# Forty-eight products that nobody reads, placed in TensorE's waits in the early slots of an RWKV-7 and squared-ReLU kernel

## The chip, the cores and the metric

One core of one Trainium2 chip. The metric is the device time of one execution in microseconds (us). The kernel before and a changed kernel are run alternately on the same chip. One traced execution of each kernel gives the profile. Its span (first to last instruction) is about 1.7 us shorter than the time of the same execution.

## The reference

Inputs `r, k, v, w, a, b` have the shape (4, 8, 768, 40): 4 sequences, 8 heads, 768 steps, 40 channels, float32.

```python
for t in range(S):
    y[:, :, t] = einsum('bhd,bhde->bhe', r_t, state)
    Sa = einsum('bhde,bhe->bhd', state, a_t)
    state = state * w_t[:, :, None, :] - einsum('bhd,bhe->bhde', Sa, b_t) + einsum('bhd,bhe->bhde', v_t, k_t)
# (B,H,S,D) -> x of 3072 x 320
h = maximum(x @ w_in, 0)          # 320 -> 2048
out = (h * h) @ w_out             # 2048 -> 320
```

## The kernel before

The sequence is cut into 24 pieces of 128 steps, which I call slots: 6 chunks of each of the 4 sequences. Slots 0 to 3 are the first chunk of each. A slot is `chain(i)`: a row of small products, each of which needs the last one's result copied out of PSUM. Other work is woven in between: preparing later slots (`early`, `rest`), rounding the second set of weights (slots 0 and 1), and from slot 2 the feed-forward network (`ffn`).

The part that the change touches, cut:

```python
def chain(i, g):
    ...
    x_ = by_head(psum(ps_c))                              # bank 1 of 2
    for h in range(H):
        mm(x_[:, h], g["A"][h % 2][:, h // 2], v_[:, h, :D], h == 0)
    ...
    nc.scalar.copy(xr[first], x_[first])
    yield
    xs = by_head(psum(ps_c))                              # bank 2 of 2
    for h in range(H):
        mm(xs[first, h], T[first, order_of(h)], xr[first, h], h == 0)
    nc.scalar.copy(xn[first, :, :D], xs[first])
    yield
    for h in range(H):
        mm(x_[second_, h], N[:, order_of(h)], xn[first, h, :D], False)
    nc.scalar.copy(xr[second_], x_[second_])
    yield
    for h in range(H):
        mm(xs[second_, h], T[second_, order_of(h)], xr[second_, h], h == 0)
    nc.scalar.copy(xn[second_, :, :D], xs[second_])
    yield
    p_ = psum(ps_c)
    for q in range(NP):
        nc.tensor.transpose(p_[:, q * 128:(q + 1) * 128], pair(xn, q), ident)
    ...                       # state, masks; the last products are RV,in_k and RX,in_b into y_
```

Each `yield` lets the weave put other work in. Some names that the profile uses: `dec` is a slot's table of decays, stored by `early` and loaded back by `rest`; `decay` is the same table while it is made for a later slot; `A`, `RV` and `RX` are products that VectorE multiplies with a triangular mask; groups named `ident,...` are transposes, and `ps_c<-ident` alone is a group of the new products; `RX,in_b` is the last product of a slot. A clock that is down, or cold, is at 0.50; full is 1.00. `T` comes from an inversion on GpSimd, once for two or four slots (`solve`). Its input is loaded by the same queue as the stores that end a slot, and behind them (in the trace before, the stores of slot 3 are issued from 299.62 us on, the loads of `half_n` from 302.57):

```python
store(t_[row:row + m_, j], t_[at:at + m_, NT], 1)      # end of chain: the token stores, four of them
...
nc.sync.dma_start(out=part[...], in_=kept[...])         # solve: loads half_n from kept_d
```

Of the kernel before, what the change touches and what calls it, by code (L numbers as in the profile page):

```python
# [17 lines left out]
def kernel(  # L18
# [24 lines left out]
    B, H, S, D = r.shape  # L43
# [26 lines left out]
    ps_c = ctx.enter_context(tc.tile_pool(name="ps_c", bufs=2, space=PSUM))  # L70
    ps_f = ctx.enter_context(tc.tile_pool(name="ps_f", bufs=2, space=PSUM))

    def psum(pool):
        name = "ps_" + pool.name[-1]
        return pool.tile([128, 512], FP32, tag=name, name=name)

    def mm(o, l_, r_, start):
        nc.tensor.matmul(o, l_, r_, start=start, stop=True, skip_group_check=True)  # L78

    def single(name, shape):  # L80
        return const.tile(shape, FP32, tag=name, name=name)

    def new(name, shape, bufs):
        return work.tile(shape, FP32, tag=name, name=name, bufs=bufs)
# [4 lines left out]
    def later(fn, steps=2):  # L89
        line.append([steps, fn])  # L90
# [7 lines left out]
    def store(out_, in_, steps=2):  # L98
        later(lambda: nc.sync.dma_start(out=out_, in_=in_), steps)  # L99

    quads = lambda t_: t_.rearrange("p (q t) -> p q t", q=NP)
    by_head = lambda t_: t_[:, :DM].rearrange("t (h d) -> t h d", h=H)
# [43 lines left out]
    ident = single("ident", [128, 128])  # L146
# [136 lines left out]
    def masked(name, bufs, l_, r_):  # L283
        res = []
        for p_ in products(l_, r_):
            t_ = new(name, [128, NP, 128], bufs)
            nc.vector.tensor_tensor(t_, p_, over4(upper), Alu.mult)  # L287
            res.append(t_)
        return res
# [150 lines left out]
    def chain(i, g):  # L440
        bb, c = order[i]
        st = states.tiles[bb]
        aT, rT, k_, b_, v_, T, N = (g[x] for x in ("aT", "rT", "k", "b", "v", "T", "N"))
        sd = g.get("sd")
        first, second_ = slice(0, HC), slice(HC, C)
        x_ = by_head(psum(ps_c))
        for h in range(H):
            mm(x_[:, h], g["A"][h % 2][:, h // 2], v_[:, h, :D], h == 0)
        if c > 0:
            for q in range(NP):  # L450
                mm(x_[:, 2 * q:2 * q + 2], aT[:, q], st[:, q, :, :D], False)
        xr = new("xr", [128, H, D], 1)
        nc.scalar.copy(xr[first], x_[first])
        yield
        xn = minus_x.next()
        xs = by_head(psum(ps_c))
        for h in range(H):
            mm(xs[first, h], T[first, order_of(h)], xr[first, h], h == 0)
        nc.scalar.copy(xn[first, :, :D], xs[first])
        yield  # L460
        for h in range(H):
            mm(x_[second_, h], N[:, order_of(h)], xn[first, h, :D], False)
        nc.scalar.copy(xr[second_], x_[second_])
        yield
        for h in range(H):
            mm(xs[second_, h], T[second_, order_of(h)], xr[second_, h], h == 0)
        nc.scalar.copy(xn[second_, :, :D], xs[second_])
        yield
        p_ = psum(ps_c)
        for q in range(NP):  # L470
            nc.tensor.transpose(p_[:, q * 128:(q + 1) * 128], pair(xn, q), ident)  # L471
        xT = turned("xnT", 1)
        nc.scalar.copy(xT, quads(p_))
        yield
        if c < NCH - 1:
            grown = psum(ps_c)[:, :NP * 2 * D].rearrange("p (q e d) -> p q e d", q=NP, e=2)
            for q in range(NP):
                mm(grown[:, q], pair(k_, q), v_[:, 2 * q:2 * q + 2, :D], q == 0)
            for q in range(NP):
                mm(grown[:, q], pair(b_, q), xn[:, 2 * q:2 * q + 2, :D], False)  # L480
            nc.vector.tensor_tensor(st[:, :, :, :D], grown, st[:, :, :, :D], Alu.add)
            ended[bb] = new(f"end{bb}", [128, NP], 1)
            nc.vector.tensor_copy(ended[bb], g["up"][:, :, C])
            yield
        rx = masked("RX", 2, xT, rT)
        yield

        y_ = quads(psum(ps_c))
        if c > 0:
            for q in range(NP):  # L490
                mm(y_[:, q], sd[:, q].rearrange("p e d -> p (e d)"), rT[:, q], q == 0)
        for m_, rows in ((g["RV"], k_), (rx, b_)):
            for q in range(NP):
                for e in range(2):
                    mm(y_[e * DP:(e + 1) * DP, q], rows[:, 2 * q + e, :], m_[e][:, q], c == 0 and q == 0 and rows is k_)
        n = i % GB
        if n == 0:
            tokens[i // GB] = new("tokens", [128, NP, GB * C], 2)
        t_ = tokens[i // GB][:, :, n * C:(n + 1) * C]
        nc.vector.tensor_tensor(t_, y_, g["up"][:, :, :C], Alu.mult)  # L500
        for j, row, h, d, m_ in gaps:
            at = (h % 2) * DP + d
            store(t_[row:row + m_, j], t_[at:at + m_, NT], 1)
        if n == GB - 1:
            later(lambda: gathered.add(i // GB), 2)
        yield
# [113 lines left out]
    for i in range(len(order)):  # L620
        bb, c = order[i]
        n, ahead = share.get(i, (TOTAL, 0))
        for _ in range(ahead):
            next(second)
            tick()
        tc.no_sync_barrier()
        parts = [(chain(i, ready.pop(i)), 9, 0, TOTAL)]
        if 1 < i + 1 < len(order):
            load(i + 1)
            ready[i + 1] = {}  # L630
            parts.append((rest(i + 1, ready[i + 1]), 9, 2, TOTAL))
        if i < B:
            parts += [(prepare(B + 2 * i), 5, 0, TOTAL - 5), (prepare(B + 2 * i + 1), 5, 5, TOTAL)]
        elif i + LEAD < len(order):
            parts.append((prepare(i + LEAD), 5, 0, TOTAL - 2))
        if i < 2:
            parts.append((some(rounding, 8 - 4 * i), 8 - 4 * i, 0, TOTAL))
        parts.append((some(second, n), n, 0, TOTAL))
        weave(*parts)
# [34 lines left out]
```

## Time and profile before

| | before |
|---|---|
| median of 4 runs beside the change | 1188.46 us (1185.67 to 1190.74) |
| span of the traced execution | 1177.1 us |
| busy: TensorE, VectorE, ScalarE, GpSimd | 85%, 42%, 20%, 62% |
| mean clock granted to TensorE | 0.917 |

The traced execution was shorter than any of the four timed ones.

Two habits of reading help here. First, the clock column gives the clock that the trace knows of, and in the first 100 us it says 1.00 although the products take their slow time: a group of 16 for `ps_w<-dec,kvT` takes 2.08 us at 67.86 us, and 1.16 us where the clock is full. The duration of a known group is the safer thermometer. Second, the bracket at the end of a timeline line gives TensorE's idle time before the group, and who ended it.

### The profile page before, as it was taken

To read this page: it belongs to the slowest core of one execution; us is meant where nothing else is said; L and a number is where in the kernel's file an instruction comes from. 1 tells how busy PE (TensorE), PEld (TensorE's weight loads), DVE (VectorE), ACT (ScalarE), POOL (GpSimd) and SP (SyncE) were. 2 spreads that over 40 slices of the span, in tenths; PEclk is the share of its full clock that TensorE was granted. 3 is DMA by queue.
4 is the path that set the end of the run, shared out by engine and by line. 5 is a ranking of instruction groups with operands and counts; after the bars stand their busy time and mean duration, and the time that the engine had idled before them with its cause. 6 is when DMAs were issued, how large, how long until landed. Compare 5 with 4: busy or idle time off the path is not lost.

```text
span 1177.1 us, 18561 instructions
## 1 busy us (share of the span) xinstructions
PE 999.4 (85%) x7248; PEld 829.6 (70%) x7248; DVE 491.1 (42%) x1008; ACT 233.5 (20%) x511; POOL 731.4 (62%) x1085
## 2 busy tenths in 40 slices
PE   4232477889999899429999989999989999999998
PEld 3121466778788687318888878788778887888886
DVE  6289576354354155005525424544233242322211
ACT  1033121211221122002112112122122121221211
POOL 4687886488488699979997059994089990000000
PEclk9997556879989899859999989999999999999999
DMA  7946645747655934244663394354353421433000
GB/s 113 169 135 182 137 110 125 146 104 160 152 99 101 170 70 86 48 94 98 109 105 101 86 155 78 87 113 101 92 90 66 77 52 51 76 64 76 3 13 12
DMA packets 261992, 114.95 MB, mean 98 GB/s; under 512 B 243472, under 2 KB 248464, under 8 KB 260368
## 3 DMA queue, kind: packets, MB, share of 16 engines
q1 hardware_dynamic: 256704, 96.98, 43.3%
q10 hardware_dynamic: 4048, 10.49, 3.1%
q0 software_dynamic: 1152, 6.29, 1.4%
q8 instruction: 57, 0.93, 0.4%
q14 instruction: 31, 0.25, 0.1%
HBM read 77.34 MB, written 35.40 MB: 96 GB/s over the span
## 4 chain that ended last, share of the span: by engine, by line
PE 61%; POOL 9%; DVE 5%; DMA 4%; SPq 2%; issue 1%; ACT 0%; POOLq 0%; DVEq 0%; ACTq 0%
PE ps_f L78 34%; PE ps_c L78 16%; PE ps_w L78 6%; POOL half_t L354 5%; POOL half_p L352 4%; PE ps_w L271 4%; DMA dec<-kept_e 2%; DMA T<-kept_t 1%; SPq L133 1%; PE ps_c L428 1%; SPq L99 1%; PE ps_c L471 1%; DVE RV L287 1%; PE ps_w L418 1%; DMA half_n<-kept_d 1%
## 5 line engine op out<-in xcount | busy, mean ns | idle before, releaser
L352 POOL TENSOR_TENSOR half_p<-half_n,half_t 128x252 f32<-128x252 f32 (+52 forms) x504 | 333.6, 662 | 169.6 <-DMA half_n<-kept_d 130.6
L354 POOL TENSOR_TENSOR half_t<-half_t,half_p 128x252 f32<-128x252 f32 (+52 forms) x504 | 366.1, 726 | 39.5
L78 PE MATMUL ps_f<-tokens,w_in 128*128 128x256 f32 x1152 | 293.1, 399 | 0.0
L523 DVE TENSOR_TENSOR hid<-ps_f,hid 128x256 f32<-128x256 f32 x192 | 80.8, 421 | 412.9 <-ACT hid L522 412.8
L78 PEld LDWEIGHTS ps_f<-tokens,w_in 128*128 128x128 f32 x1152 | 216.0, 198 | 31.2 <-issue 0.4
L78 PE MATMUL ps_f<-w_out,hid 128*128 128x320 f32 x768 | 221.0, 437 | 0.0
L78 PEld LDWEIGHTS ps_f<-w_out,hid 128*128 128x128 f32 x768 | 140.7, 190 | 53.9 <-issue 0.2
L522 ACT ACTIVATE hid<-ps_f 128x256 f32<-128x256 f32 x192 | 73.8, 384 | 244.9 <-PE ps_f L78 244.9
L78 PE MATMUL ps_c<-xr,T 64*64 64x40 f32 x768 | 59.4, 239 | 54.1 <-DMA T<-kept_t 52.7
L78 PEld LDWEIGHTS ps_c<-xr,T 64*64 64x64 f32 x768 | 53.7, 147 | 70.3 <-issue 68.2
L78 PEld LDWEIGHTS ps_c<-in_v,A 128*128 128x128 f32 x384 | 50.5, 206 | 17.1 <-DVE w_out L230 14.7
L78 PE MATMUL ps_c<-in_v,A 128*128 128x40 f32 x384 | 49.1, 290 | 14.3 <-DVE w_out L230 14.3
L78 PE MATMUL ps_w<-dec,kvT 40*128 40x128 f32 x384 | 32.4, 316 | 27.3 <-DVE kvT L394 27.2
L78 PEld LDWEIGHTS ps_w<-dec,kvT 40*128 40x128 f32 x384 | 27.3, 215 | 32.2 <-DVE kvT L394 29.2
L78 PE MATMUL ps_w<-decay,bT 40*128 40x128 f32 x352 | 36.8, 340 | 15.4 <-DVE decay L312 13.8
L319 ACT COPY N<-ps_w 128x512 f32<-128x512 f32 x48 | 25.8, 589 | 119.6 <-PE ps_w L78 71.9
L500 DVE TENSOR_TENSOR tokens<-ps_c,dec 128x512 f32<-128x512 f32 x24 | 16.5, 686 | 72.6 <-PE ps_c L78 70.7
L271 PE MATMUL ps_w<-ident,in_w 128*128 128x128 f32 x96 | 19.1, 333 | 32.4 <-DMA in_w<-in_w_dram 31.0
L78 PEld LDWEIGHTS ps_w<-decay,bT 40*128 40x128 f32 x352 | 31.3, 237 | 21.0 <-issue 12.9
L287 DVE TENSOR_TENSOR RX<-ps_w,upper 128x512 f32<-128x512 f32 x48 | 30.8, 682 | 27.0 <-PE ps_w L78 27.0
L78 PEld LDWEIGHTS ps_c<-minus_x,N 64*64 64x64 f32 x384 | 28.1, 153 | 15.3 <-issue 8.5
L307 DVE RECIPROCAL decay<-decay 128x256 f32<-128x256 f32 x22 | 38.3, 1739 | 0.0
(110 smaller groups left out, 1205.8 us busy)
## 6 DMA issues: line engine op xcount, KB each, us to landing
kept_e<-decay SPq DMA_DIRECT2D x22, 780.0 KB
dec<-kept_e SPq DMA_DIRECT2D x22, 780.0 KB
half_n<-kept_d SPq DMA_DIRECT2D x24, 256.0 KB
hid<-in_moe_w_out_dram ACTq DMA_DIRECT2D x16, 320.0 KB
half_n<-kept_d SPq DMA_DIRECT2D x8, 512.0 KB
kept_t<-half_t POOLq DMA_DIRECT2D x4, 1024.0 KB, 5.2
T<-kept_t SPq DMA_DIRECT2D x64, 64.0 KB
in_w<-in_w_dram SPq DMA_DIRECT2D x24, 160.0 KB
```

Of the source, the lines that this page charges most:

```text
L78: nc.tensor.matmul(o, l_, r_, start=start, stop=True, skip_group_check=True)
L99: later(lambda: nc.sync.dma_start(out=out_, in_=in_), steps)
L133: nc.sync.dma_start(out=t_[:, :, :D], in_=src[bb, :, c * C:(c + 1) * C, :].rearrange("h t d -> t h d"))
L271: nc.tensor.transpose(p_[:, q * 128:(q + 1) * 128], pair(x_, q), ident)
L287: nc.vector.tensor_tensor(t_, p_, over4(upper), Alu.mult)
L307: nc.vector.reciprocal(down[:, :, MID + 1:C + 1], up[:, :, MID + 1:C + 1])
L319: nc.scalar.copy(t_[:, e * NP:(e + 1) * NP], p_)
L352: eng.tensor_tensor(p_, ns[s // Q][:, s % Q, s % Q + 1:].unsqueeze(1).to_broadcast([128, n, m_]), ts[:, :n, s:s + 1].to_broadcast([128, n, ...
L354: eng.tensor_tensor(ts[:, :n, s + 1:], ts[:, :n, s + 1:], p_, Alu.subtract)
L500: nc.vector.tensor_tensor(t_, y_, g["up"][:, :, :C], Alu.mult)
L522: nc.scalar.activation(h_, p_, Act.Relu)
L523: nc.vector.tensor_tensor(h_, p_, h_, Alu.mult)
```

## The change

The intent is to fill TensorE's waits for ScalarE's copies, so that its clock stays up: in this trace it falls six times from 161.8 to 332.5 us, each time with TensorE idle for 2.1 to 2.8 of the 3.41 us before. Each of four places in `chain` gets three products of the unit matrix with itself, in slots 0 to 3. They write columns 384 to 511 of a PSUM bank, of which only the first 320 are used, and they alternate between the two banks so that they never write the bank that ScalarE is reading.

```diff
-        x_ = by_head(psum(ps_c))
+        bank = psum(ps_c)
+        x_ = by_head(bank)
+        other = None
+        def busy(b_):
+            for _ in range(3 if i < B else 0):
+                mm(b_[:, 384:], ident, ident, b_ is other)
 ...
-        xs = by_head(psum(ps_c))
+        other = psum(ps_c)
+        xs = by_head(other)
+        busy(other)                 # group 1, before the first product with T
 ...
+        busy(bank)                  # group 2, before the product with N
 ...
+        busy(other)                 # group 3, before the second product with T
 ...
+        busy(bank)                  # group 4, before the transposes of x
         p_ = psum(ps_c)
```

## The prediction

> **What bounds the kernel now.** I read the page first: engines, the row of clock slices, the chain that ended last. Then a table of windows, one for each of slots 0 to 3 (I take a slot from its first product of v with A to the end of its last product), then TensorE's timeline inside the slots, and last GpSimd's timeline and the chain around 390 us.
>
> ```profile
> span 1177.1 us, 18561 instructions
> PE 999.4 (85%) x7248; PEld 829.6 (70%) x7248; DVE 491.1 (42%) x1008; ACT 233.5 (20%) x511; POOL 731.4 (62%) x1085
> PEclk9997556879989899859999989999999999999999
> PE 61%; POOL 9%; DVE 5%; DMA 4%; SPq 2%; issue 1%; ACT 0%; POOLq 0%; DVEq 0%; ACTq 0%
> ```
>
> TensorE carries the chain. The low clock digits, 7 5 5 6 8 7, stand in the fourth to ninth slice of 29.4 us (88 to 265 us); slots 0 to 3 lie at 118 to 302 us. By slot (columns: us, busy of PE, weight load, DVE, ACT, POOL, then the clock):
>
> ```profile
> 118.00:166.00 48.00, 27.69 (x172) 24.21 (x172) 28.41 (x62) 8.73 (x19) 40.86 (x77) 0.54 0.50 117
> 166.00:209.00 43.00, 33.09 (x236) 29.86 (x236) 29.81 (x62) 9.99 (x21) 29.56 (x61) 0.61 0.59 123
> 209.00:262.00 53.00, 46.08 (x322) 40.58 (x324) 25.26 (x53) 10.97 (x25) 38.28 (x70) 0.83 0.64 135
> 262.00:302.00 40.00, 38.83 (x304) 31.33 (x305) 20.80 (x43) 7.27 (x15) 30.92 (x63) 0.93 0.65 137
> ```
>
> Slot 0 runs at half clock with TensorE idle 20 of 48 us; slot 3 is nearly all TensorE at full clock. So the same insertion meets an idle engine in one and a full one in the other. The places where the twelve products go:
>
> ```profile
> 132.21 1.93 PE L78 MATMUL ps_c<-minus_x,N 64*64 64x40 f32 x16 [5.37 <-ACT minus_x L459]
> 143.78 1.09 PE L471 MATMUL ps_c<-ident,minus_x 128*128 128x128 f32 x4 [4.46 <-ACT minus_x L467]
> 175.62 1.92 PE L78 MATMUL ps_c<-minus_x,N 64*64 64x40 f32 x16 [0.51 <-ACT minus_x L459]
> 182.75 1.09 PE L471 MATMUL ps_c<-ident,minus_x 128*128 128x128 f32 x4 [0.60 <-ACT minus_x L467]
> 231.09 1.12 PE L78 MATMUL ps_c<-minus_x,N 64*64 64x40 f32 x16 [0.51 <-ACT minus_x L459]
> 240.53 2.08 PE L78 MATMUL ps_w<-dec,kvT 40*128 40x128 f32 x16 [2.53 <-DVE kvT L394]
> 270.60 1.12 PE L78 MATMUL ps_c<-xr,T 64*64 64x40 f32 x16
> 274.00 1.12 PE L78 MATMUL ps_c<-minus_x,N 64*64 64x40 f32 x16
> 282.50 1.16 PE L78 MATMUL ps_w<-dec,kvT 40*128 40x128 f32 x16
> ```
>
> The reader is to see the bracket shrink from 5.37 us to none: only in slot 0 is the wait for PSUM long; in slot 3 other work already fills it. The same lines show the clock: one group of 16 takes 2.08 us at 240.53 and 1.16 us at 282.50.
>
> Why early slots count at all is in GpSimd's inversions, each gated by the end of a slot:
>
> ```profile
> 218.31 0.29 POOL L352 TENSOR_TENSOR half_p<-half_n,half_t 128x63 f32<-128x63 f32 x1 [15.59 <-DMA half_n<-kept_d]
> 309.73 0.29 POOL L352 TENSOR_TENSOR half_p<-half_n,half_t 128x63 f32<-128x63 f32 x1 [8.35 <-DMA half_n<-kept_d]
> 396.88 0.29 POOL L352 TENSOR_TENSOR half_p<-half_n,half_t 128x63 f32<-128x63 f32 x1 [4.09 <-DMA half_n<-kept_d]
> ```
>
> Each inversion waits for a load issued behind the token stores that end slots 1, 3 and 5. The one at 396.88 runs to 511 us and releases slot 8 at 523. So a microsecond gained by the end of slot 3 reaches the end of the kernel almost whole (slot 5 follows slot 3, and the inversion of 309.73 moves with it); one lost does too.
>
> [...]the clock is 0.50 from 100.4 to 158.5, then changes at 161.9, 196.0, 202.7, 206.2, 209.6, 216.4, 240.2, 250.5, 260.8, 267.6 and 332.5 us, all whole multiples of about 3.41 us apart. What the trace adds is that the falls came with idle of only 2.0 to 2.9 us in the window, and that continuous work from 168.7 to 175.1 us did not warm it[...].[...] the window that ended in the rise of 196.0 was half transposes (x8 from 194.4 on).[...] three products of 256 columns in 1.46 us warm and 2.93 us cold.
>
> **The change, part by part.** Nothing is removed or reordered: comparing the built programs, VectorE, ScalarE, GpSimd and the queues have the same instructions in the same order; TensorE has 16 groups of three more, 48 products, two records each. The first group of a slot stands before the first product with T, the second before N, the third before the second T, the fourth before the four transposes of x.
>
> Cost of one: four products of 128x128 by 128 columns (ps_c<-rT,sd, 346.88 to 347.96) took 1.08 us, so 0.27 us warm; cold I take 0.5 us (the ratio 2.93 to 1.46). A group is 0.8 us warm, 1.5 cold; a slot 3.2 or 6.
>
> - Slot 0, cold: groups in idle of 2.48, 5.37, 1.36 and 4.46 us. Only the third is 0.15 us too long: +0.2. Groups 3 and 4 with the transposes ahead of them fill about 134 to 141 us[...], so the clock rises about 138 to 141; but the rest of the 4.46 us is idle again and it mostly falls before the work at 146 to 152.4, for which VectorE waits 3.53 us. If it stayed warm, that wait would be about 2.6 us shorter; I give that 0.3: -0.8.
> - Slot 1, cold: idle of none, 0.51, none and 0.60, so the groups push TensorE back by 4 to 5 us until 182 to 187. Yet the next result is used by VectorE, which stands waiting for the load of dec (to 184.34) and then has its own queue up to the mask at 189.46, so little of this shows. In return the third group follows 2.8 us of transposes, and by 185 the clock should be full. Then the stretch 190.2 to 196.9 (4.3 us of products and 2 of transposes, cold, on VectorE's path) falls to about half, less what VectorE adds: about 2.4 us, taken at seven tenths: -1.7.
> - Slot 2: four warm groups are 3.2 us and the idle there is 0.51 + 2.53 = 3.04 us, waiting for the load of dec, so they cost 0.1. The idle that let the clock fall at 240.2 is filled, so the chain from 240.5 to 250.4 (9.9 us busy at 0.50) runs warm: TensorE saves 4.5 us, VectorE's masks leave about 3. The clock would not fall in every execution[...]: about eight tenths of it, -2.4 with the 0.1 in it.
> - Slot 3: full clock, no idle. All four groups lie on the path: +3.2.
>
> Sum: +0.2 - 0.8 - 1.7 - 2.4 + 3.2 = -1.5 us, from 1189.1 to 1187.6. Against that stands what I can't trace[...] (one cold window at 332.5 to 339.3 costs about 3 us when it comes). That can go either way; more warmth before a slot is a little likelier than less, so I say 1187.
>
> **Rivals.** (a) The clock is the main thing and the groups hold it full from slot 0 on. For: 27.7 and 33.1 us of cold work in slots 0 and 1 would shrink by up to 28 us of busy time. Against: ScalarE and VectorE own slot 0's waits (reciprocals at 1.7 us each, rounding of weights), and a window with 2 to 3 us idle cools it again. With it 1172 to 1180. (b) The groups are only work: clock unchanged, slots 1 and 3 pay 4 and 3.2 us: 1193 to 1196. For: in slot 3 it is so. (c) All is hidden, since GpSimd's inversions set slot 8: against it, GpSimd idles 15.59, 8.35 and 4.09 us before them; it limits gains by the end of slot 5 to about 2.4 us beyond those by slot 3. 1189.
>
> **Range and chances.** The three runs before spread over 3 us. The terms above are uncertain by 2 to 3 us each, more on the side of gain in slots 0 and 1: 1178 to 1195. Faster by 2% means below 1165.3, which needs nearly all that (a) could give: 0.03. Slower by 2% means above 1212.9, over twice all 48 products at the warm 13 us: 0.02. Within: 0.95.
>
> **What would show it.** Right: TensorE has 96 more records and 13 to 20 us more busy time less what warmth saves; slot 0's end does not move; the clock in slot 1 is above 0.61 and in 240 to 250 near 1.00; slot 3 is about 3 us longer; the shift at the start of the inversion at 309.73 equals that at the end of the span to 2 us. Wrong: a clock near 1.00 throughout slot 0, a slot 3 that grows by less than 1 us, or a gain that arises after slot 5.

## The result, and the profile after

| | before | changed |
|---|---|---|
| median of 4 runs | 1188.46 us | 1182.86 us (1182.48 to 1184.00) |
| ratio | | 0.9956 (0.9933 to 0.9979) |
| span of the traced execution | 1177.1 us | 1181.2 us |

A ratio is the mean time of the changed kernel's runs over that of the other's of the same rounds, so it is not quite the ratio of the medians. The brackets are a 95% interval. The time lies in the predicted range, 4 us below the predicted 1187. Two later comparisons gave 0.9998 and 0.9982 (below), so the first one may have been on the lucky side.

The page of the changed kernel:

```profile
span 1181.2 us, 18751 instructions
PE 1008.1 (85%) x7344; PEld 838.8 (71%) x7344; DVE 489.9 (41%) x1008; ACT 233.3 (20%) x511; POOL 731.5 (62%) x1085
PEclk8555557889989999759999999999989999999999
```

TensorE has 96 more records, as foretold, and 8.7 us more busy time. The other engines have the same instructions. The same four slots, with the columns of the prediction's table (us, busy of TensorE, weight load, VectorE, ScalarE, GpSimd, clock, DMA); the limits lie, as in the prediction's table, at the group `ps_w<-decay,bT` that runs after each slot's last product (and at 118 us for slot 0), moved to where it starts in this trace:

```profile
118.00:165.00 47.00, 33.34 (x196) 29.62 (x195) 28.10 (x60) 8.72 (x19) 39.96 (x75) 0.50 0.51 115
165.00:209.00 44.00, 34.86 (x260) 31.94 (x260) 29.95 (x63) 9.88 (x21) 30.46 (x63) 0.69 0.55 120
209.00:258.00 49.00, 44.32 (x346) 38.99 (x348) 25.57 (x53) 10.87 (x25) 34.48 (x64) 0.93 0.76 147
258.00:304.00 46.00, 44.83 (x324) 37.37 (x325) 20.70 (x43) 7.27 (x15) 34.94 (x69) 0.86 0.56 119
```

Slot 2 is 4 us shorter than in the trace before, at clock 0.93 for 0.83. Slot 3 is 6 us longer, at 0.86 for 0.93. TensorE's timeline of the changed kernel shows both, and below it the start of slot 3 before:

```profile
131.61 1.93 PE L78 MATMUL ps_c<-minus_x,N 64*64 64x40 f32 x16 [3.79 <-ACT minus_x L471]
...
183.78 0.94 PE L78 MATMUL ps_c<-ident 128*128 128x128 f32 x6
...
190.25 1.11 PE L271 MATMUL ps_w<-ident,in_w 128*128 128x128 f32 x4 [2.46 <-DVE A L287]
...
240.66 1.16 PE L78 MATMUL ps_w<-dec,kvT 40*128 40x128 f32 x16 [0.30 <-DVE kvT L394]
...
253.79 1.04 PE L78 MATMUL ps_c<-RX,in_b 128*64 128x128 f32 x16
257.81 2.08 PE L78 MATMUL ps_w<-decay,bT 40*128 40x128 f32 x16 [2.97 <-DVE decay L312]
259.82 2.93 PE L78 MATMUL ps_f<-tokens,w_in 128*128 128x256 f32 x6
262.54 3.47 PE L78 MATMUL ps_c<-in_v,A 128*128 128x40 f32 x16
265.81 1.09 PE L271 MATMUL ps_w<-ident,in_w 128*128 128x128 f32 x4
266.70 2.77 PE L78 MATMUL ps_f<-tokens,w_in 128*128 128x256 f32 x6
269.26 1.49 PE L78 MATMUL ps_c<-ident 128*128 128x128 f32 x6
```

```profile
261.73 2.08 PE L78 MATMUL ps_w<-decay,bT 40*128 40x128 f32 x16 [2.97 <-DVE decay L312]
263.74 2.93 PE L78 MATMUL ps_f<-tokens,w_in 128*128 128x256 f32 x6
266.46 2.45 PE L78 MATMUL ps_c<-in_v,A 128*128 128x40 f32 x16
```

At 131.61 the wait of 5.37 us has become 3.79 us, and the slot ends where it did (162.8 us for 163.4): in slot 0 the wait is filled in part and nothing is won. At 183.78 the group takes 0.94 us, so the clock is full; at 190.25 it has fallen again in the 2.46 us that TensorE waits for VectorE's masks, and slot 1 ends at 207.1 us as before (207.0). At 240.66 the wait of 2.53 us for the load of dec is filled to 0.30 us, the clock holds, and slot 2 ends at 254.8 for 258.8 us. Then TensorE waits 2.97 us for VectorE's decays, a wait that both kernels have. Here the clock falls, and it stays down from 257.4 to 271.2 us although TensorE hardly rests; before, it was down from 260.8 to 267.6. What slot 2 gained, slot 3 gave back.

### The profile page after: what moved, and what is told of

Same layout as the page of the kernel before. It is cut to its first block, busy times and chain, and to the rows that moved or that the text cites. A ratio compares the mean times of both kernels' runs of the same rounds, so it can differ in the third digit from the quotient of the medians.

```text
span 1181.2 us, 18751 instructions
## 1 busy us (share of the span) xinstructions
PE 1008.1 (85%) x7344; PEld 838.8 (71%) x7344; DVE 489.9 (41%) x1008; ACT 233.3 (20%) x511; POOL 731.5 (62%) x1085
## 4 chain that ended last, share of the span: by engine, by line
PE 61%; POOL 9%; DVE 5%; DMA 4%; SPq 3%; issue 1%; ACT 0%; POOLq 0%; DVEq 0%; ACTq 0%
PE ps_f L78 34%; PE ps_c L78 16%; PE ps_w L78 6%; POOL half_t L354 5%; POOL half_p L352 4%; PE ps_w L271 4%; DMA dec<-kept_e 1%; SPq L133 1%; DMA half_n<-kept_d 1%; DMA T<-kept_t 1%; PE ps_c L428 1%; PE ps_c L486 1%; DVE RV L287 1%; PE ps_w L418 1%; SPq L99 1%
## 5 line engine op out<-in xcount | busy, mean ns | idle before, releaser
L352 POOL TENSOR_TENSOR half_p<-half_n,half_t 128x252 f32<-128x252 f32 (+52 forms) x504 | 334.0, 663 | 170.3 <-DMA half_n<-kept_d 131.3
L78 PEld LDWEIGHTS ps_c<-in_v,A 128*128 128x128 f32 x384 | 51.5, 209 | 17.2 <-DVE w_out L230 14.7
L287 DVE TENSOR_TENSOR A<-ps_w,upper 128x512 f32<-128x512 f32 x48 | 30.7, 680 | 22.0 <-PE ps_w L78 22.0
L271 PEld LDWEIGHTS ps_w<-ident,in_w 128*128 128x128 f32 x96 | 14.0, 181 | 34.9 <-issue 27.2
```

The lines of the kernel that those rows point to most:

```text
L78: nc.tensor.matmul(o, l_, r_, start=start, stop=True, skip_group_check=True)
L271: nc.tensor.transpose(p_[:, q * 128:(q + 1) * 128], pair(x_, q), ident)
L287: nc.vector.tensor_tensor(t_, p_, over4(upper), Alu.mult)
L352: eng.tensor_tensor(p_, ns[s // Q][:, s % Q, s % Q + 1:].unsqueeze(1).to_broadcast([128, n, m_]), ts[:, :n, s:s + 1].to_broadcast([128, n, ...
```

## The experiments

Theory: the products act through the clock; they gain in slot 2, and the gain is lost at the next fall. Rivals: slot 3's own products are what loses (as predicted); the delay or the filling, not the clock, is what gains; or the whole is scatter. All twelve runs gave the right result. To compare traces I read off for each where slots end (end of the last RX,in_b) and when the clock was down. The ends are read from TensorE's timeline, the clock in steps of 0.2 us from windows:

| run | end of slot 1 | of slot 2 | of slot 3 | slot 3 takes | clock down between 235 and 350 us | span |
|---|---|---|---|---|---|---|
| before, first trace | 207.0 | 258.8 | 297.8 | 39.0 | 240.4-250.6, 260.8-267.6, 332.6-339.4 | 1177.1 |
| before again (e1) | 208.7 | 260.4 | 297.1 | 36.7 | 242.0-252.2, 334.0-341.0 | 1178.8 |
| slot 3 alone (e2) | 208.2 | 260.1 | 301.8 | 41.7 | 241.6-252.0, 262.2-269.0, 337.2-344.0 | 1182.7 |
| changed, first trace | 207.1 | 254.8 | 300.1 | 45.3 | 257.4-271.2, 336.0-342.8 | 1181.2 |
| changed again (f1) | 207.8 | 254.6 | 295.2 | 40.6 | 258.4-261.8, 330.0-340.2 | 1174.8 |
| changed, third (g4) | 208.3 | 255.8 | 301.1 | 45.3 | 258.6-272.2, 337.2-344.0 | 1179.2 |
| slots 0 to 2 (e3) | 207.5 | 255.2 | 299.4 | 44.2 | 257.8-275.0, 336.4-343.2 | 1180.9 |
| small products (e4) | 207.3 | 255.2 | 303.7 | 48.5 | 258.0-278.6, 340.0-350.2 | 1185.6 |
| slot 2 alone (f2) | 207.1 | 254.8 | 299.0 | 44.2 | 257.4-274.6, 336.0-342.8 | 1177.7 |
| slot 2, ends of 1 and 2 (f3) | 208.6 | 260.1 | 296.9 | 36.8 | 242.4-252.6, 334.6-341.4 | 1175.8 |
| the same and slot 4 (f4) | 207.7 | 259.3 | 296.5 | 37.2 | 241.0-251.2, 333.2-343.4 | 1177.5 |
| slot 2 and its end (g1) | 208.8 | 256.6 | 293.8 | 37.2 | never | 1172.3 |
| the same and slot 3 (g2) | 209.2 | 261.4 | 300.3 | 38.9 | 243.4-253.8, 335.6-345.8 | 1181.1 |
| longer in slot 2, both ends (g3) | 207.7 | 255.3 | 292.6 | 37.3 | 330.0-336.8 | 1175.0 |

Slot 1 ends within 2.2 us of the same time in all of them. The span follows the end of slot 3: in all fourteen traces it is 878 to 882 us longer.

**The kernel before once more, parts of the change, and another kind of product.** `e1_before_again` is the kernel before without any edit.

> The kernel before, unchanged, once more. Its first trace had a span of 1177.1 us, while its four timed runs lie at 1185.7 to 1190.7, so that trace may be a lucky one. [...]the new trace has a span of 1183 to 1189 us and more or longer cold stretches between 240 and 340 us than the first. If the profiled execution is simply shorter than the timed ones by some fixed cost, the span is again within 2 us of 1177. Time: ratio 1.000 within 0.002 in either case.

Measured: 1183.36 us, ratio 0.9989 (0.9937 to 1.0042), span 1178.8 us. The expectation of a longer span failed: the second trace is nearly as short as the first. But the time scattered far more than the four first runs had shown: eleven runs of the kernel before on this chip went from 1174.53 to 1191.56 us. The first trace lies in the lower part of a wide spread; there is no fixed offset.

`e2_only_slot3`:

```diff
-            for _ in range(3 if i < B else 0):
+            for _ in range(3 if i == 3 else 0):
```

> The twelve products in slot 3 alone. Theory (warmth gained in slots 0 to 2, slot 3 pure cost): ratio 1.0027, 3.2 us slower than before. Rival A (slot 3's groups also keep a stretch of slot 3 warm, or a later one): ratio 0.997 to 1.000.

Measured: 1182.93 us, 0.9977 (0.9926 to 1.0028). The time can't tell 1.0027 from 0.998. In the trace slot 3 takes 41.7 us, 2.7 us more than in the first trace of before with a cold stretch of the same 6.8 us.

`e3_slots_0_to_2`, with `i < 3` in the same place:

> The groups in slots 0 to 2, none in slot 3. Theory: the measured gain of 5.3 us plus the 3.2 us of slot 3, so ratio about 0.9928, 8.5 us faster than before. Rival A: same as the changed kernel or less gain, 0.995 to 0.998.

Measured: 1183.81 us, 0.9987 (0.9937 to 1.0038). My theory of the prediction fell here: without slot 3's products slot 3 still takes 44.2 us, hardly less than the 45.3 us with them. So slot 3 is not long because of its own products. Its cold stretch is: 257.8 to 275.0 us, 17 us, where the first trace of before had 6.8 us. In the changed kernel the stretch ends at 271.2 us, just behind slot 3's first group (269.26 to 270.75, shown above).

`e4_small_products` changes the kind of product, not the time that a group takes:

```diff
-            for _ in range(3 if i < B else 0):
-                mm(b_[:, 384:], ident, ident, b_ is other)
+            for _ in range(6 if i < B else 0):
+                mm(b_[:HC, 384:384 + D], ident[:HC, :HC], ident[:HC, :D], b_ is other)
```

> In place of each group of three 128x128 products with 128 columns, six of a 64x64 array with 40 columns, which take about the same time (1.43 us cold, 0.79 warm by the products with T)[...]. Theory (the gain is the clock): the clock stays down as before in slots 1 and 2 and nothing is gained, so the time is that of before plus the cost of slots 1 and 3, ratio 1.002 to 1.006. Rival B (the gain comes from the delay that the products put between TensorE's other work, or from idle simply being filled with anything): ratio about 0.9955 as with the change.

Measured: 1182.88 us, 0.9983 (0.9927 to 1.0040). The trace has two answers. In slot 2 the small products do as well as the large ones: the clock does not fall at 240 us (it is 1.00 until 258.0) and the slot ends at 255.2 us. So here, against my expectation, small products were enough to hold the clock. In slot 1 they did not raise it, as I had expected: it stayed down until 196.6 us, where the changed kernel's first rise is at 182.4. Nor did they raise it in slot 3: after the fall at 258.0 us it stays down for 20.6 us, the longest of all traces, with TensorE busy 20.45 of the 20.60 us, as the window shows:

```profile
258.00:278.60 20.60, 20.45 (x99) 16.59 (x100) 5.57 (x12) 2.68 (x6) 18.36 (x29) 0.50 0.80 159
```

This trace is of an execution of 1187.3 us, one of the slow end of the spread, and its slot 3 takes 48.5 us.

**The change again, and filling the next wait too.** `f1_after_again` is the changed kernel without any edit.

> The changed kernel once more, since the kernel before scattered from 1174.5 to 1191.6 us in eleven runs of one chip and the first comparison had only four runs of each. If the gain of 0.44% is real, the ratio is 0.994 to 0.997; if it was the scatter of before, 0.998 to 1.002.

Measured: 1180.57 us against 1180.60 us, 0.9998 (0.9968 to 1.0028). The 0.44% was not there on this chip. Its trace, set beside the first one of the same program, shows how much chance is in a single execution. Here the clock came back after 3.4 us:

```profile
257.59 1.43 PE L78 MATMUL ps_w<-decay,bT 40*128 40x128 f32 x16 [2.97 <-DVE decay L312]
258.95 2.93 PE L78 MATMUL ps_f<-tokens,w_in 128*128 128x256 f32 x6
261.67 1.92 PE L78 MATMUL ps_c<-in_v,A 128*128 128x40 f32 x16
```

The products of v with A take 1.92 us here and 3.47 us in the first trace, after the same wait of 2.97 us. The clock changes at other times: here at 258.4 and 261.8 us, and the full-size products of the network (2.93 us) lie nearly whole between the two. In the first trace the fall is at 257.5 us, these products run from 259.82 to 262.75, and the clock comes back only at 271.1 us. That the place of these products in the 3.4 us steps decides it is my estimate from these two traces. In the other traces, where the fall comes 2.1 us after slot 2's last product (before, e2) the clock is down for 6.8 us, at 2.6 to 2.9 us (changed, g4, e3, e4, f2) for 13.6 to 20.6 us, at 3.7 us (f1) for 3.4 us. In e1 TensorE was busy for only 1.42 us from 258.98 to 262.39 us and no fall followed; in the first trace of before it was busy for 1.35 us from 257.41 to 260.82 us, and the clock fell. One program: slot 3 takes 40.6 or 45.3 us, and the span 1174.8 or 1181.2 us.

`f2_only_slot2` has `i == 2` in place of `i < B`.

> The twelve products in slot 2 alone, where in the traces slot 2 ended 4 us earlier (RX,in_b ends at 254.8 to 255.2 us with the products, 258.8 to 260.4 without). Theory (the wait for dec is filled, the clock does not fall at 240 us; slot 3 then begins with a longer cold stretch, which gives most of it back): slot 2's last product ends at about 255, slot 3's at 299 to 301, ratio 0.998 to 1.001. Rival (slot 2's gain stays and slot 3's loss was its own products): slot 3's last product ends at 293 to 295 and the ratio is 0.995 to 0.997.

Measured: 1180.25 us, 0.9996 (0.9965 to 1.0028). The theory's numbers hold: slot 2 ends at 254.8 us, slot 3 at 299.0 us, and nothing is left of the 4 us. No product stands in slot 3 here, so the rival is out as the cause.

`f3_slot2_and_ends` adds six products behind the last product of slots 1 and 2, where TensorE waits for VectorE's decays:

```diff
-            for _ in range(3 if i < B else 0):
+            for _ in range(3 if i == 2 else 0):
 ...
-            grown = psum(ps_c)[:, :NP * 2 * D].rearrange("p (q e d) -> p q e d", q=NP, e=2)
+            last = psum(ps_c)
+            grown = last[:, :NP * 2 * D].rearrange("p (q e d) -> p q e d", q=NP, e=2)
 ...                                  # behind the products RV,in_k and RX,in_b
+        for _ in range(6 if i in (1, 2) else 0):
+            mm(last[:, 384:], ident, ident, False)
```

> Twelve products in slot 2 and six more after the last product of slots 1 and 2, where TensorE waits 2.9 us for the decays of VectorE and the clock falls in every trace (at 209.6 to 211.2 and at 257 to 262). Theory (what the change gains in slot 2 is lost again at that fall): the clock holds from slot 1's end on, the cold stretch after slot 1 (6.8 us) and the one at the start of slot 3 go, slot 3's last product ends at 290 to 294, and the ratio is 0.991 to 0.995, since the inversion on GpSimd limits what reaches the end. Rival (the fall is not due to that idle time, or the six products delay the next one by as much as they save): slot 3 ends at 297 or later, ratio 0.998 or more.

Measured: 1177.51 us against 1180.60 us, 0.9978 (0.9945 to 1.0011). ("In every trace" in the expectation is not so: e1 has no fall at 257 to 262 us.) Half of the theory came true: both falls behind the slots are gone (no cold stretch at 209 or 260 us) and slot 3 takes 36.8 us. But the fall at 242 us is back, and slot 2 ends at 260.1 us:

```profile
237.92 0.83 PE L78 MATMUL ps_c<-ident 128*128 128x128 f32 x6
238.59 0.60 PE L486 MATMUL ps_c<-ident,minus_x 128*128 128x128 f32 x4
241.58 1.35 PE L78 MATMUL ps_w<-dec,kvT 40*128 40x128 f32 x16 [2.39 <-DVE kvT L394]
```

With a full clock behind slot 1, TensorE reached the wait for dec 1 us earlier (its last group at 237.92 for 239.08 us in the changed kernel), while the load came 0.9 us later (VectorE starts its product with dec at 240.83 for 239.91 us). The wait was 2.39 us in place of 0.30 and the clock fell. A saved microsecond became part of a wait, and the fall cost about four: slot 2 ends 51.5 us after slot 1, for 47.7 in the changed kernel.

`f4_slot2_ends_slot4` adds groups 3 and 4 in slot 4 to f3:

```diff
-        def busy(b_):
-            for _ in range(3 if i == 2 else 0):
+        def busy(b_, at=(2,)):
+            for _ in range(3 if i in at else 0):
 ...
-        busy(other)
+        busy(other, (2, 4))
 ...
-        busy(bank)
+        busy(bank, (2, 4))
         p_ = psum(ps_c)
```

> As the run before, and the third and fourth group in slot 4 as well, where TensorE waits 2.25 us for the load of dec and the clock falls (332 to 337 us in every trace) for one or two windows. Theory: slot 4 is 2 to 3 us shorter than in the run before, ratio 0.989 to 0.994. Rival (slot 4 has no room: the groups cost 1.6 us and the clock falls anyway): slot 4 as long or longer.

Measured: 1178.77 us, 0.9986 (0.9958 to 1.0015). ("In every trace" is not so here either: the clock fell at 330.0 us in f1 and at 340.0 in e4.) A miss: the clock fell at 333.2 us all the same, for 10.2 us, and slot 4 takes 56.1 us (296.5 to 352.6) against 54.3 (296.9 to 351.2) in f3. As the rival said, there was no room.

**The gain kept.** `g1_slot2_and_its_end` is f3 with the six products behind slot 2 alone, so that slot 2 begins as late as before:

```diff
-        for _ in range(6 if i in (1, 2) else 0):
+        for _ in range(6 if i == 2 else 0):
```

> Twelve products in slot 2 and six behind its last product, nothing in slots 0, 1 and 3. Slot 2 then begins as late as before (the six behind slot 1 had let it begin 1 to 2 us earlier, which opened the wait for dec again). Theory (the 4 to 5 us of slot 2 are lost at the fall of the clock at 257 us): slot 2's last product ends at about 255, the clock does not fall at 257 to 262, slot 3 takes 36 to 38 us, its last product ends at 291 to 293, and the ratio is 0.993 to 0.997. Rival (whatever ends slot 3 is not the clock but VectorE or the loads): it ends at 296 or later, ratio 0.998 to 1.001.

Measured: 1174.18 us against 1185.29 us, 0.9926 (0.9881 to 0.9970). It is faster than both kernels, with 18 products instead of 48; against the change (1181.90 us) the medians are 7.7 us apart. It was measured beside four runs of the kernel before. The trace:

```profile
255.51 1.04 PE L78 MATMUL ps_c<-RX,in_b 128*64 128x128 f32 x16
256.48 1.60 PE L78 MATMUL ps_c<-ident 128*128 128x128 f32 x12
259.53 1.16 PE L78 MATMUL ps_w<-decay,bT 40*128 40x128 f32 x16 [1.44 <-DVE decay L312]
260.62 1.56 PE L78 MATMUL ps_f<-tokens,w_in 128*128 128x256 f32 x6
262.02 1.88 PE L78 MATMUL ps_c<-in_v,A 128*128 128x40 f32 x16
```

These are the lines of 253.79 to 262.54 of the changed kernel, with the wait of 2.97 us cut to 1.44 us. The next product was not delayed, since it still waits for VectorE; and it, the network's products and those of v with A take 1.16, 1.56 and 1.88 us in place of 2.08, 2.93 and 3.47. Slot 3 takes 37.2 us. The rival (VectorE or the loads set the end of slot 3) is out. At slot 5 the gain is 5.8 us (it ends at 379.1 for 384.9 us). Less than that reaches the end, because of GpSimd:

```profile
392.35 1.80 POOL L340 MEMSET half_t<- 128x2048 f32 x1 [7.97 <-DMA kept_t<-half_t]
```

The inversion for slots 8 to 11 starts at 394.6 us, only 2.3 us earlier than in the first trace of before (396.9), since the store of the inversion before it took 7.97 us to release its buffer (2.54 us there). The span is 4.8 us shorter. Only about 2.7 of these go back to the inversion: slot 8's first product with T starts at 520.9 for 523.5 us. After it the clock came back within 4.8 us in g1 and within 10.4 us in the first trace of before; that the other 2 us come from there is likely, but not shown.

`g2_slots23_and_end2` is g1 with `i in (2, 3)` for the groups of three.

> The run before with the twelve products of slot 3 as well. If they are pure cost where the clock is full, as predicted, slot 3 is 3.2 us longer than in the run before (39 to 41 us) and the ratio 0.002 to 0.003 higher. Rival (they are hidden, or keep something warm): slot 3 within 1 us of the run before.

Measured: 1176.54 us, 0.9946 (0.9902 to 0.9990), 0.0020 above g1; the intervals overlap. In the trace slot 3 has a full clock in both, and takes 38.9 us with its products and 37.2 without. That is the clean price of the twelve: 1.7 us, about half of the predicted 3.2 (the five traces with no products in slot 3 and a full clock there, e1, f3, f4, g1 and g3, agree to 0.6 us). Part of it went into a wait for dec that g1 has there, as a line of g1 and one of g2 show:

```profile
278.15 1.16 PE L78 MATMUL ps_w<-dec,kvT 40*128 40x128 f32 x16 [0.59 <-DVE kvT L394]
```

```profile
284.98 1.16 PE L78 MATMUL ps_w<-dec,kvT 40*128 40x128 f32 x16
```

In this trace the same groups did not hold the clock in slot 2. After slot 1 it was down for 3.4 us only (6.8 in g1), TensorE came to the wait for dec earlier, as in f3, waited 1.78 us there (0.40 in g1), and slot 2 ended at 261.4 us. So the gain of slot 2 is not there in every execution. It also answers the rival of delay and filling: in f3, f4 and g2 the products stood in slot 2, the clock fell all the same, and slot 2 gained nothing (it ends at 259.3 to 261.4 us).

`g3_longer_slot2_both_ends` is f3 with groups 3 and 4 of slot 2 made six products long (`busy(other, 6)`, `busy(bank, 6)`).

> Six products behind the last product of slots 1 and 2, and in slot 2 groups of 3, 3, 6 and 6, so that the wait for dec is filled although slot 2 begins earlier. Theory: full clock from the end of slot 1 to 330 us, slot 2 ends at 253 to 256, slot 3 at 290 to 293; but slot 3's inversion can't start before that of slot 1 has ended, about 303 us, so at most 6 us reach the end: ratio 0.992 to 0.996. Rival: as for the first run of this call.

Measured: 1177.46 us, 0.9958 (0.9912 to 1.0003). The clock was full from 207 to 330 us, slot 2 ended at 255.3 and slot 3 at 292.6 us, all as the theory said. It did not beat g1: its inversion for slots 8 to 11 starts at the same 394.6 us. Why its median lies 3.3 us above g1's is not shown; in its trace the clock came back 10.2 us after slot 8's first product with T (4.8 in g1), one execution each.

`g4_after_third` is the changed kernel without any edit.

> The changed kernel a third time. The first comparison gave 0.9956 (0.9933 to 0.9979), the second, on another chip, 0.9998 (0.9968 to 1.0028). If the effect is one small number, about 0.998, this gives 0.995 to 1.001.

Measured: 1181.90 us against 1185.29 us, 0.9982 (0.9937 to 1.0026).

## Why the prediction was right or wrong

The time was right; of the terms that made it, several were wrong and cancelled, so that the sum came close is in part luck. In the first pair of traces slots 0 and 1 gained nothing that lasted, slot 2 gained 4.0 us and slot 3 lost 6.2.

- *What bounds the kernel, and how a microsecond of slot 3 reaches the end.* Right. In the pair of first traces the inversion after slot 3 starts 2.8 us later (312.5 for 309.7) and the span is 4.1 us longer. In g1 it starts 3.5 us earlier and the span is 4.8 us shorter. Both lie within the 2 us that I had allowed, and the span follows slot 3's end within 4.3 us over fourteen traces. The limit by GpSimd beyond slot 3 showed in g1. (One reading was off without effect: the inversion of 396.88 us runs to 514 us, not 511.)
- *Slot 0: +0.2 - 0.8.* The end hardly moved, as foretold: 162.8 for 163.4 us, of which 0.3 us is an earlier start. But the step behind the -0.8 failed: the clock was to rise at 138 to 141 us, and in the changed trace it is 0.50 until 182.4 us, with TensorE busy for 6.15 of the 7.00 us from 134 to 141. TensorE still waits there, 3.79 us for ScalarE and 2.90 us for VectorE.
- *Slot 1: -1.7.* Failed. The clock did rise as predicted, at 182.4 us (0.69 over the slot, for 0.61), but it fell again at 189.2 us in a wait for VectorE's masks, so the stretch from 190.2 us ran cold as before. I had named this queue of VectorE and not followed what its 2.46 us do to the clock. Slot 1 gains nothing in any of the traces.
- *Slot 2: -2.4.* The cause was right: the wait for dec is filled (2.53 us to 0.30), the clock holds (1.00 from 240.5 to 250.5 us), slot 2 ends about 4 us earlier. The term was too small (2.4 for 4.0 us), and it was not final: the prediction followed the gain to the end of slot 2 and not into the next idle time, of 2.97 us, in which the clock falls.
- *Slot 3: +3.2, "full clock, no idle".* Failed as a description, and this is the step that cost most. The cold stretch from 260.8 to 267.6 us was in the trace before, and I had taken it for something that the change doesn't touch. The prediction's own table has 0.93 for this slot. The stretch grew to 14 to 21 us in five of the six traces with groups in slot 2 whose slot 2 ended early and whose end was not filled (changed, g4, e3, e4, f2); in the sixth, f1, it lasted 3.4 us. Where the clock is alike in both, the twelve products cost 1.7 us (g2 against g1) to 2.7 us (e2 against the first trace of before), not 3.2.
- *Rivals.* (a), full clock from slot 0 on, did not come about. (b), only work, is out by slot 2. (c), hidden by GpSimd, is out by g1.
- *Signs.* The 96 records, the end of slot 0, the clock in slot 1 and in 240 to 250 us (full) and the shift of the inversion came as foretold. "Slot 3 is about 3 us longer" did not: it was 6.2 us longer, and not by its products alone.

Is the change faster at all? The three comparisons gave 0.9956, 0.9998 and 0.9982. Weighted by their intervals that is 0.997, some 3 us. I don't call its size settled, as the first and the second hardly agree. The scatter may have changed too: of 36 runs of the kernel before, 14 took over 1185 us, up to 1193.45; none of the 16 of the changed kernel did (1175.57 to 1184.00). I chose that limit after seeing the times, and no run was made to test it. Why the slow executions of before are slow stays open: no trace of that kernel fell on one. That e4's slow trace has the longest cold stretch, and that f1 and the first trace of the same program differ by one, makes the times at which the clock falls and comes back a likely cause. For the kernel before that is my estimate, and not shown.

## What to carry to other kernels

In this kernel, filler for TensorE paid where its idle time would have let the clock fall and where work that sets the end followed (slot 2 and its end, 0.9926); in slots 0 and 1 it was lost, and in slot 3, which is full, it cost 1.7 to 2.7 us. Follow the clock past the place that you fill, to the next idle time: here the gain was mostly given back there until that one was filled too, and an earlier arrival at a load that came no earlier opened a new wait. One trace of each kernel is not a comparison here: three traces of the changed kernel had spans of 1174.8 to 1181.2 us, with the clock down for 3.4 to 13.8 us at the start of slot 3. Take several, and compare the ends of slots before comparing spans.

## What the traces showed of the clock

- Falls came behind time that was idle in part. In the first trace of before and in that of the changed kernel the times between two changes of the clock are whole multiples of 3.41 us. In the six falls of before from 161.8 to 332.5 us TensorE was busy for 0.65 to 1.35 of the 3.41 us ahead of the fall; at the changed kernel's fall of 189.2 us, for 1.66. In g1, with 1.60 us of filler in what was a wait of 2.97 us, it was busy for 2.09 us from 256.00 to 259.41 us, and the clock held.
- A busy TensorE did not always bring the clock back. The changed kernel stayed cold from 257.4 to 271.2 us with 13.39 us of busy time, e4 from 258.0 to 278.6 us with 20.45. The work of 168.7 to 175.1 us in the kernel before, products with 40 moving columns or on a 64x64 array and 1.1 us of transposes, fills all 6.40 us and did not raise it; e4's small products kept it up in slot 2 all the same. In f1 the 3.41 us up to 261.75, filled for the most part by the network's products of 128x128 with 256 columns (2.93 us), ended in a rise. What a rise needs was not shown beyond these cases.
- A stretch that was mostly FP32 transposes (`nc.tensor.transpose`) was followed by a full clock. In f2 that of 175.6 to 179.0 us held 0.8 us of 64x64 products and 2.6 us of transposes, and the clock was 1.00 in the next 3.41 us:

```profile
175.58:178.99 3.41, 3.41 (x20) 3.11 (x19) 3.34 (x5) 0.42 (x1) 3.02 (x6) 0.50 1.22 184
178.99:182.40 3.41, 1.83 (x21) 1.43 (x20) 1.10 (x1) 0.42 (x1) 2.96 (x6) 1.00 0.96 245
```

- Within one program the falls differ from execution to execution. Three traces of the changed kernel had cold stretches of 13.8, 3.4 and 13.6 us at the same place and spans of 1181.2, 1174.8 and 1179.2 us.
